# Half a sequence's six score units in one row, one pool of seven banks, and a shorter weight rounding, in a hash attention and SwiGLU kernel

## The chip, the cores and the metric

The kernel runs on one core of a Trainium2 chip. The metric is the device time of one execution in microseconds (us). The kernel before takes 1043.42 us, the median of three runs (1043.08 to 1043.81).

## What is computed

Attention over 4 batches, 8 heads, 768 positions and 64 dimensions, in which a query sees only the keys that fall into the same of 64 hash buckets (the signs of six projections). Its output, 3072 rows of 512, goes through a SwiGLU feed-forward block of 1536 hidden columns.

```python
q_bits = (np.einsum('bhsd,dk->bhsk', q, proj) > 0)
k_bits = (np.einsum('bhsd,dk->bhsk', k, proj) > 0)
mask = q_bucket[:, :, :, None] == k_bucket[:, :, None, :]   # bucket: the bits as a number
scores = np.where(mask, scale * np.matmul(q, k.transpose(0, 1, 3, 2)), -1e9)
attn = np.exp(scores - np.max(scores, axis=-1, keepdims=True))
attn = attn / (np.sum(attn, axis=-1, keepdims=True) + 1e-09)
x = np.matmul(attn, v)          # then (B, H, S, D) -> (B*S, H*D)
g = x @ w_gate
out = (g / (1 + np.exp(-g)) * (x @ w_val)) @ w_out
```

Inputs are fp32, but the three weight matrices come as 8-byte words (the double precision numbers as they are), and the kernel makes fp32 of them on the chip.

## The kernel before

**Attention.** The 32 (batch, head) pairs are taken two heads at a time: 16 *pairs*, four to a batch. A pair has two *halves* of 384 queries, and a half has six *units* of 128 keys (`units`, `NCH = 6`), so there are 192 units. For a unit `score(u)` issues four matmul groups: `kT` by `qT` in fp32 for each head (64 rows each, the two heads in two row tiles), and the hash bits `kb` by `qb` in bf16, which add a large negative number wherever the buckets differ. Two `exp` on ScalarE bring the two scores tiles into one of a ring of tiles `A`. `attend(u)` multiplies `v` by `A` (two heads in two 64-column tiles) and adds into one PSUM bank `av` over six units; after the sixth a copy on ScalarE (`avs`) frees it. `add(u)` adds the `A` tiles on VectorE into `acc`, five additions a half. `norm(u)` multiplies `acc` by ones (`sum`, which gives the sum over keys in every row), takes the reciprocal on VectorE, adds a small term `e` and writes the normalised `xT`.

**Front work of a pair.** `front(n)` yields eight steps: four transposes of `q` and `k` (TensorE, `tps`, then a copy on ScalarE) and four hash projections (`hps`, then a Sign on ScalarE and for `k` a scaling on VectorE). After the fourth pair VectorE transposes instead and one small set of matmuls makes all four projections.

**Weights.** `prepare()` is a generator of small VectorE steps that `prepare_on(count)` advances; every piece is 128 x 512 words, 36 pieces in all. `narrow(i)` turns a piece from doubles to fp32 in four VectorE steps: FLOOR (line 289), a shift (291), an integer addition (294) and the sign (297). With two of them it issues ScalarE steps for the next piece (`scalar_step`, lines 275 and 280), and with the last it asks GpSimd for the DMA of the words some pieces ahead (`load_words`). After every four pieces eight additions (line 325, `form`) make the sums that the fast multiplication needs.

**Feed-forward.** It uses Strassen's scheme (7 products instead of 8) on both multiplications. When the last pair of a batch is normalised, `push_ffn(b)` queues its *atoms*: sets of 14 `up` atoms (each one product for one of the gate and the value blocks of 256 hidden columns, added into one of the banks `a`, `b`, `c`), then chunks of seven `po` atoms for the second multiplication. Elementwise additions (`plus`) stand between them, and the first combinations of `xT` (`first`) are made on VectorE.

**Order.** The order is written out by hand: an engine does its instructions in the order in which the loops issue them. The first loop (units 0 to 47, the first four pairs, eight halves) goes by two units: score two, attend the two before, `norm` of a half that ended an iteration earlier, additions, two front steps, three preparation steps. There is no FFN work yet. The second loop (units 48 to 191, 24 halves) goes by half: score two, attend the four left over, four preparation steps, `norm` of the half before, score two, attend two, score two, and then 14 atoms of FFN work (or chunks of `po`) with additions, front steps and preparation steps between them. Weights are prepared until `MOVE` (unit 84).

**Banks and tiles.** PSUM has three pools: four banks for scores (`score_tile`; the `b` and `c` tiles of `up` and one `po` tile too), one for `av`, three for everything else (`bank`: transposes, hashes, sums, `up` and `po`). `A` is a ring of four tiles, six from unit 48 on.

Of the kernel before, what the change touches and what calls it, by code (L numbers as in the profile page):

```python
# [18 lines left out]
def kernel(  # L19
# [11 lines left out]
    nc = tc.nc  # L31
# [24 lines left out]

    FLOOR = 2.0**-15

    konst = ctx.enter_context(tc.tile_pool(name="konst", bufs=1))
# [6 lines left out]
    dram = ctx.enter_context(tc.tile_pool(name="dram", bufs=1, space=bass.MemoryType.DRAM))  # L66
    sc_ps = ctx.enter_context(tc.tile_pool(name="sc_ps", bufs=4, space=PSUM))
    av_ps = ctx.enter_context(tc.tile_pool(name="av_ps", bufs=1, space=PSUM))
    mm_ps = ctx.enter_context(tc.tile_pool(name="mm_ps", bufs=3, space=PSUM))

    ctx.enter_context(tc.manual_schedule())

    def bank(name):
        return mm_ps.tile([P, 512], FP32, tag="mm", name=name)

    def score_tile(name):
        return sc_ps.tile([P, 512], FP32, tag="sc", name=name)

# [80 lines left out]
    nc.vector.tensor_tensor(rules, rules, ident.unsqueeze(1).to_broadcast([P, 2, P]), op=ALU.mult)  # L159
    columns = konst.tile([P, 3], FP32, tag="columns", name="columns")  # L160
    nc.vector.tensor_reduce(out=columns[:, 0:2], in_=rules, axis=AX.X, op=ALU.add)
    nudge, times_k, two = (columns[:, x : x + 1] for x in range(3))
    nc.vector.memset(two, 2.0)

# [104 lines left out]

    def scalar_step(i, low):  # L270

        if i < len(pieces) and not low:
            nc.scalar.activation(pieces[i][0], words[i][:, :, 1].bitcast(FP32), AF.Abs)  # L275
        elif i < len(pieces):
            t = words[i]
            top = t.rearrange("p f w -> p (f w)").bitcast(U16)
            top = top.rearrange("p (f w) -> p f w", w=4)[:, :, 1]
            nc.scalar.activation(t[:, :, 0].bitcast(FP32), top, AF.Identity, bias=two,  # L280
                                 scale=2.0**-35 * (1 + 2.0**-17))

    def narrow(i):
        t, w = words[i], pieces[i][0]
        lo, hi = t[:, :, 0], t[:, :, 1]
        wi = w.bitcast(I32)


        nc.vector.tensor_single_scalar(w, w, FLOOR, op=ALU.max)
# [43 lines left out]
    def prepare():  # L333
        for n in range(2 * DF // PIECE):
            for j in range(NJ):
                if n + j == 0:
                    for low in (False, True):
                        scalar_step(0, low)
                yield from narrow(n * NJ + j)
            for pair in range(2):  # L340
                yield from form(n, pair)
        for f in range(NF):
            yield from narrow(2 * NJ * DF // PIECE + f)
        t2, t3, t4 = down_t
        for o, x, y, op in ((t3, b22, b12, ALU.subtract), (b12, b12, b11, ALU.subtract),
                            (t2, b22, b12, ALU.subtract), (t4, b21, t2, ALU.subtract)):
            while o is t4 and not progress["late"]:
                yield True
            for a in range(0, NFP, 2):
                nc.vector.tensor_tensor(o[:, a : a + 2], x[:, a : a + 2], y[:, a : a + 2], op=op)  # L350
                yield True
# [17 lines left out]

    def front_bank(name):  # L370

        return bank(name)

    def front(n):


        def transpose(name, half):
            if (name, n) not in T:
                T[name, n] = opnd.tile([P, S], FP32, tag=name + "T", name=name + "T")
            ps = front_bank("tps")  # L380
            for i in range(CH):
# [15 lines left out]
        def hash_bits(name, half):  # L397
            ps = front_bank("hps")
            nc.tensor.matmul(ps[:, 0:HQ], hash_w, T[name, n][:, half * HQ : (half + 1) * HQ],  # L399
# [5 lines left out]
        def hash_blocks():  # L405

            tile_ = front_bank("hps")
            for i, (name, half) in enumerate((name, half) for name in "kq" for half in range(2)):
# [39 lines left out]
    def weights(u):  # L448
        if u < LATE:
            return ring[u % RING]  # L450
        return ((early_ring if u < MOVE else late_ring) + ring)[(u - LATE) % (RING + 2)]

    def score(u):
        n, half, c = units[u]
        qs = slice(half * HQ, (half + 1) * HQ)
        ks = slice(c * P, (c + 1) * P)
        sc = [score_tile("sc")[:, 0:HQ] for _ in range(2)]
        for x, start in ((T, True), (bits, False)):
# [77 lines left out]
    def up_strassen(x, b, first):  # L536
# [14 lines left out]
        def both(i):  # L551
# [13 lines left out]
            def step(at):  # L565
                n, g = divmod(at, 2)
                my = now[g]
                if n == 0:
                    my["a"] = bank("up")[:, 0:HQ]
                    while first:  # L570
                        first.pop(0)()
                if at == 2:
                    for name in "cb":
                        for w in range(2):
                            now[w][name] = score_tile("up")[:, 0:HQ]
                block, to, xs = (
# [34 lines left out]
    def down_strassen(out_of):  # L611
# [22 lines left out]
        def chunk(i):  # L634
            now = {}

            def step(n):
                a11, a12, s3, a22 = parts(i, slice(None))
                if n == 0 and i == 0:
                    while next(preparing, None):  # L640
                        pass
                    for which in (1, 2, 3):
                        combine(0, which, 1)
                if n < 2:
                    now["ab"[n]] = bank("po")[:, 0:HD]
                elif n == 3:
                    now["c"] = score_tile("po")[:, 0:HD]
                if n == 0:
                    o = wraw.tile([P, PIECE, 2], I32, tag="words", name="o")
                    o = o.rearrange("p f w -> p (f w)").bitcast(FP32)  # L650
# [42 lines left out]


    steps = front(0)
    for _ in range(5):
        steps.pop(0)()
    N = len(units)
    per = 2 * NCH
    credit = ahead = 0.0  # L700
    left = []
    due = []
    for u in range(0, LATE, 2):
        n, at = divmod(u, per)
        if at == (4 if n == 0 else 0):
            steps.extend(front(n + 1))
        if at == per - 2:
            load(n + 2)
        score(u)
        score(u + 1)  # L710
        for x in left:
            attend(x)
        while due:
            norm(due.pop(0))
        for x in left:
            add(x)
            if units[x][2] == NCH - 1:
                due.append(x)
        left = [u, u + 1]
        for _ in range(2):  # L720
            if (u < 4 or u % per >= 2) and steps:
                steps.pop(0)()
        prepare_on(2 if u < 4 else 3)

    assert not steps
    for x in left:
        add(x)
    for u in range(LATE, N + NCH, NCH):  # L730
        if u < N:
            n, half, _ = units[u]
            if u == MOVE:
                progress["late"] = True
                for t in late_ring:
                    nc.gpsimd.memset(t[:, :, HQ:AW], 1.0)
            score(u)
            score(u + 1)
        for x in left:
            attend(x)  # L740
        prepare_on(4)
        ended = [x for x in due + left if units[x][2] == NCH - 1]
        due = []
        if u != LATE:
            for x in ended:
                norm(x)
        if u == N:
            break
        score(u + 2)
        score(u + 3)  # L750
        if u == LATE:
            for x in ended:
                norm(x)
        prepare_on(3)
        attend(u)
        attend(u + 1)
        score(u + 4)
        score(u + 5)
        prepare_on(4)
        add(u)  # L760
        add(u + 1)
        left = [u + c for c in range(2, NCH)]
        more = [lambda x=x: add(x) for x in left]
        if half == 0 and n + 1 < len(pairs):
            steps = front(n + 1)
            more[1:1] = [steps.pop(0)]
            more[3:3] = [steps.pop(0)]
        elif n + 1 < len(pairs):
            more[1:1] = [steps.pop(0)]
            if n + 2 < len(pairs):  # L770
                load(n + 2)
        chores = [lambda: first and first.pop(0)() and None for _ in first] + more

        credit += 14 if n < 2 * NP else 15.75
        end = True
        while atoms and (credit > 0 or not end):
            size, atom, end = atoms.pop(0)
            credit -= size
            atom()
            ahead += 0.85 * size  # L780
            prepare_on(int(ahead))
            ahead %= 1
            for _ in range(size):
                if chores:
                    chores.extend(chores.pop(0)() or [])
        while chores:
            chores.extend(chores.pop(0)() or [])
    for _, atom, _ in atoms:
# [33 lines left out]
```

## Time and profile before

| | |
|---|---|
| Median of three runs | 1043.42 us |
| The profiled execution | 1042.24 us |
| its span (first to last instruction) | 1040.5 us, so 1.74 us lie around it |
| TensorE clock granted | 0.998 of full speed |
| Reciprocal of the sum, VectorE | 32 x 2.56 us |
| Addition into `acc`, VectorE | 128 x 0.95 us |
| `exp` of one head's scores, ScalarE | 0.49 us each |

The page's second part divides the span into 40 slices of 26 us and gives each engine's busy share in tenths. Its fourth part follows the chain of work that ended last back from the end. Busy times are of one profiled execution. Matmuls overlap in their pipeline, so what a group of them costs is read best from one start to the next.

Five of the costliest groups, with busy time, mean duration in ns and, after the bar, the idle time before them:

```
L461 PE MATMUL sc<-qT,kT 64*128 64x384 f32 x768 | 168.0, 509 | 0.3
L464 ACT ACTIVATE A<-sc 128x384 f32<-128x384 f32 x288 | 120.8, 493 | 78.7 <-PE sc L461 62.6
L501 DVE RECIPROCAL r<-sum 128x384 f32<-128x384 f32 x32 | 81.8, 2556 | 103.9 <-PE sum L498 103.9
L488 DVE TENSOR_TENSOR acc<-acc,A 128x768 f32<-128x768 f32 x128 | 121.7, 951 | 6.4
L473 PE MATMUL av<-A,vraw 128*64 128x386 f32 x576 | 104.0, 496 | 0.0
```

### The profile page before, as it was taken

How to read it: one execution, taken by the hardware profiler on the slowest of the kernel's cores; microseconds unless marked ns; L12 is line 12 of the kernel's file. 1: busy time of each engine (PE TensorE's matmuls, PEld its weight loads, DVE VectorE, ACT ScalarE, POOL GpSimd, SP SyncE). 2: the span in 40 equal slices, each digit the busy share in tenths (PEclk: the TensorE clock that was granted, in tenths of full speed). 3: DMA queues.
4: the chain of work that ended last, by engine and by line, in shares of the span. 5: the costliest groups of instructions: out<-in, count | busy, mean ns of one | idle time of the engine just before them, and what ended most of it. 6: DMA issues, size and time to landing. Idle time of an engine off the chain costs nothing.

```text
span 1040.5 us, 12461 instructions
## 1 busy us (share of the span) xinstructions
PE 1029.3 (99%) x4597; PEld 604.8 (58%) x4597; DVE 628.9 (60%) x1044; ACT 424.2 (41%) x905; POOL 100.2 (10%) x192
## 2 busy tenths in 40 slices
PE   9999899999999999999999999999999999999998
PEld 4444345555456674555557666554545777555687
DVE  4899989989994435654566345455655442534521
ACT  7676637566542413534352422533535211222200
POOL 2122222221000000000000000000000000111000
PEclk9999999999999999999999999999999999999999
DMA  7565475865322122242411213241222000333101
GB/s 233 125 215 190 130 190 190 213 214 176 99 86 51 37 50 71 88 100 86 103 47 51 41 36 92 69 95 54 87 71 71 21 21 21 111 102 104 38 25 36
DMA packets 113885, 99.90 MB, mean 96 GB/s; under 512 B 86977, under 2 KB 97217, under 8 KB 113825
## 3 DMA queue, kind: packets, MB, share of 16 engines
q0 software_dynamic: 19104, 73.28, 22.0%
q1 hardware_dynamic: 93920, 25.64, 11.1%
q8 instruction: 36, 0.59, 0.2%
q10 hardware_dynamic: 800, 0.20, 0.1%
q14 instruction: 25, 0.20, 0.1%
HBM read 81.79 MB, written 17.30 MB: 95 GB/s over the span
## 4 chain that ended last, share of the span: by engine, by line
PE 90%; DVE 2%; DMA 0%; issue 0%; ACT 0%; ACTq 0%; DVEq 0%
PE up L530 42%; PE po L530 21%; PE sc L461 13%; PE av L473 11%; PE sum L498 2%; PE hps L409 1%; DVE r L501 1%; DMA words<-in_moe_w_val_dram 0%; DVE acc L488 0%; DVE room L325 0%; PE hps L399 0%; DVE acc L484 0%; PE tps L382 0%; DVE xT L504 0%; ACT A L464 0%
## 5 line engine op out<-in xcount | busy, mean ns | idle before, releaser
L530 PE MATMUL up<-xT,room 128*128 128x384 f32 x768 | 265.2, 492 | 4.2 <-ACT room L275 4.2
L530 PEld LDWEIGHTS up<-xT,room 128*128 128x128 f32 x768 | 144.5, 191 | 113.0 <-issue 7.9
L530 PE MATMUL up<-xc,room 128*128 128x384 f32 x576 | 197.5, 486 | 0.0
L461 PE MATMUL sc<-qT,kT 64*128 64x384 f32 x768 | 168.0, 509 | 0.3
L530 PEld LDWEIGHTS up<-xc,room 128*128 128x128 f32 x576 | 109.4, 190 | 76.3
L464 ACT ACTIVATE A<-sc 128x384 f32<-128x384 f32 x288 | 120.8, 493 | 78.7 <-PE sc L461 62.6
L501 DVE RECIPROCAL r<-sum 128x384 f32<-128x384 f32 x32 | 81.8, 2556 | 103.9 <-PE sum L498 103.9
L488 DVE TENSOR_TENSOR acc<-acc,A 128x768 f32<-128x768 f32 x128 | 121.7, 951 | 6.4
L534 DVE TENSOR_TENSOR c<-c,up 128x384 f32<-128x384 f32 x72 | 39.8, 553 | 138.3 <-PE up L530 138.0
L310 POOL DMA_DIRECT2D room<-ram x96 | 51.8, 540 | 689.6 <-PE up L530 678.2
L461 PEld LDWEIGHTS sc<-qT,kT 64*128 64x128 f32 x768 | 67.0, 186 | 72.6 <-issue 30.3
L473 PE MATMUL av<-A,vraw 128*64 128x386 f32 x576 | 104.0, 496 | 0.0
L662 ACT COPY o<-po 128x256 f32<-128x256 f32 x48 | 17.9, 372 | 191.9 <-PE po L530 191.9
L534 DVE TENSOR_TENSOR o<-o,po 128x256 f32<-128x256 f32 x36 | 15.2, 421 | 109.9 <-issue 51.5
L516 ACT ACTIVATE th<-c 128x384 f32<-128x384 f32 x72 | 37.6, 523 | 101.6 <-DVE c L534 101.4
L473 PEld LDWEIGHTS av<-A,vraw 128*64 128x64 f32 x576 | 37.1, 136 | 57.4 <-issue 56.0
L461 PE MATMUL sc<-qb,kb 64*128 64x384 bf16 x384 | 67.3, 323 | 0.2 <-DVE kb L394 0.2
L530 PE MATMUL po<-wo,hid 128*128 128x256 f32 x288 | 67.0, 382 | 0.0
L530 PE MATMUL po<-wo,room 128*128 128x256 f32 x288 | 66.3, 380 | 0.0
L530 PE MATMUL po<-room,hid 128*128 128x256 f32 x288 | 66.1, 379 | 0.0
L590 ACT COPY c<-up 128x384 f32<-128x384 f32 x72 | 34.4, 478 | 66.0 <-PE up L530 65.9
L530 PEld LDWEIGHTS po<-wo,hid 128*128 128x128 f32 x288 | 54.0, 190 | 11.6 <-DVE room L534 3.8
(112 smaller groups left out, 1033.3 us busy)
## 6 DMA issues: line engine op xcount, KB each, us to landing
room<-ram POOLq DMA_DIRECT2D x48, 512.0 KB, 4.6
room<-ram POOLq DMA_DIRECT2D x48, 384.0 KB, 4.0
vraw<-in_v_dram SPq DMA_DIRECT2D x16, 384.0 KB, 3.5
ram<-room POOLq DMA_DIRECT2D x12, 512.0 KB, 3.9
out_dram<-o SPq DMA_DIRECT2D x48, 128.0 KB, 1.7
qraw<-in_q_dram SPq DMA_DIRECT2D x48, 96.0 KB, 3.2
kraw<-in_k_dram SPq DMA_DIRECT2D x46, 96.0 KB, 3.3
words<-in_moe_w_out_dram POOLq DMA_DIRECT2D x8, 512.0 KB, 4.0
```

The source lines that it names most:

```text
L310: nc.gpsimd.dma_start(places[k % 2][:, PARTS[go], :], ram[k % NG][:, PARTS[go], :])
L461: nc.tensor.matmul(sc[h], x["k", n][rows, ks], x["q", n][rows, qs], start=start, stop=not start)
L464: nc.scalar.activation(weights(u)[:, h, 0:HQ], sc[h], AF.Exp, scale=SCALE)
L473: nc.tensor.matmul(ps[h * D : (h + 1) * D, 0:AW], raws["v", n][:, h, c, :], a[:, h, :], start=c == 0, stop=c == NCH - 1)
L488: nc.vector.tensor_tensor(acc[n, half], acc[n, half], a[:, :, 0:HQ], op=ALU.add)
L498: nc.tensor.matmul(ps[h * D : (h + 1) * D, 0:HQ], ones, t[:, h, :], start=True, stop=True)
L501: nc.vector.reciprocal(r, ps[:, 0:HQ])
L516: nc.scalar.activation(th, g, AF.Tanh, scale=0.5)
L530: nc.tensor.matmul(ps, a, x, start=start and i == 0, stop=i == len(pairs_) - 1, skip_group_check=True)
L534: nc.vector.tensor_tensor(o, a, b, op=op)
L590: nc.scalar.copy(tile_of(g, spot), c)
L662: nc.scalar.copy(o, c)
```

## The change

- **One loop for all units, by half.** A half's six `score` calls stand in a row with its additions between them, then its six `attend` calls, then preparation steps, then its own `norm`. In the first 48 units four front steps are spread before and after the `attend` calls and the preparation steps are eight (six in the very first half). From unit 48 on the atoms follow, with front steps and 0.7 preparation steps for each unit of atom size. No unit is scored ahead of the half before it any more, and none is attended in a later half.
- **Banks.** The pools of four and three banks become one pool of seven, from which every tile but `av` is taken. The six tiles of an `up` pair are all taken at its first atom, the three of a `po` chunk at its first.
- **Tiles `A`.** The ring has six tiles from the start, one for each unit of a half.
- **Weight rounding.** `narrow` has three VectorE steps (shift, sign, integer addition); FLOOR is gone. ScalarE has three steps instead of two for a piece: a scaled copy, an addition of 2^23 and a subtraction of it into an integer.
- **Loads.** `load(n + 2)` stands after the `attend` calls of a pair's second half.

The diff, cut:

```diff
-    sc_ps = ctx.enter_context(tc.tile_pool(name="sc_ps", bufs=4, space=PSUM))
     av_ps = ctx.enter_context(tc.tile_pool(name="av_ps", bufs=1, space=PSUM))
-    mm_ps = ctx.enter_context(tc.tile_pool(name="mm_ps", bufs=3, space=PSUM))
+    banks = ctx.enter_context(tc.tile_pool(name="ps", bufs=7, space=PSUM))
...
     def bank(name):
-        return mm_ps.tile([P, 512], FP32, tag="mm", name=name)
-
-    def score_tile(name):
-        return sc_ps.tile([P, 512], FP32, tag="sc", name=name)
+        return banks.tile([P, 512], FP32, tag="ps", name=name)
...
-    def scalar_step(i, low):
+    def scalar_step(i, k):
...
+        if k == 0:
+            nc.scalar.activation(w, t[:, :, 1].bitcast(FP32), AF.Copy, scale=2.0**-112)
+        elif k == 1:
+            nc.scalar.activation(lo.bitcast(FP32), top, AF.Identity, bias=whole,
+                                 scale=2.0**-13 * (1 + 2.0**-17))
+        else:
+            nc.scalar.activation(lo, lo.bitcast(FP32), AF.Identity, bias=unwhole)
...
-        nc.vector.tensor_single_scalar(w, w, FLOOR, op=ALU.max)
-        yield True
         nc.vector.tensor_single_scalar(wi, wi, 3, op=ALU.logical_shift_left)
-        scalar_step(i + 1, False)
-        yield True
-        nc.vector.tensor_tensor(wi, wi, lo, op=ALU.add)
-        scalar_step(i + 1, True)
+        scalar_step(i + 1, 0)
         yield True
         nc.vector.scalar_tensor_tensor(out=wi, in0=hi, scalar=-(1 << 31), in1=wi,
                                        op0=ALU.bitwise_and, op1=ALU.bitwise_or)
+        scalar_step(i + 1, 1)
+        yield True
+        nc.vector.tensor_tensor(wi, wi, lo, op=ALU.add)
+        scalar_step(i + 1, 2)
         load_words(i)
         yield True
...
     def weights(u):
-        if u < LATE:
-            return ring[u % RING]
-        return ((early_ring if u < MOVE else late_ring) + ring)[(u - LATE) % (RING + 2)]
+        return ((early_ring if u < MOVE else late_ring) + ring)[u % NCH]
...
-                if n == 0:
-                    my["a"] = bank("up")[:, 0:HQ]
+                if at == 0:
+                    for name in "cba":
+                        for w in range(2):
+                            now[w][name] = bank("up")[:, 0:HQ]
...
+    for u in range(0, N, NCH):
+        n, half, _ = units[u]
+        gating = u >= LATE
...
+        for c in range(NCH):
+            score(u + c)
+            if u == 0 and c in (1, 2, 4):
+                steps.pop(0)()
+            if c:
+                add(u + c)
+        if not gating:
+            if half == 0:
+                steps = front(n + 1)
+            for _ in range(2):
                 steps.pop(0)()
-        prepare_on(2 if u < 4 else 3)
...
+        for c in range(NCH):
+            attend(u + c)
+        if half == 1 and n + 2 < len(pairs):
+            load(n + 2)
+        if not gating:
+            for _ in range(2):
+                steps.pop(0)()
+        prepare_on(6 if u == 0 else 8)
+        norm(u + NCH - 1)
+        if not gating:
+            continue
+        chores = []
+        if n + 1 < len(pairs):
+            if half == 0:
+                steps = front(n + 1)
+                chores = [None, steps.pop(0), None, steps.pop(0)]
+            else:
+                chores = [None, steps.pop(0)]
...
-            ahead += 0.85 * size
+            ahead += 0.7 * size
             prepare_on(int(ahead))
```

More of the change, by code (lines that the diff above doesn't have):

```diff
@@ L55 @@
     EPS = 2.0**-100
-    FLOOR = 2.0**-15
     konst = ctx.enter_context(tc.tile_pool(name="konst", bufs=1))
@@ L159 @@
     nc.vector.tensor_tensor(rules, rules, ident.unsqueeze(1).to_broadcast([P, 2, P]), op=ALU.mult)
-    columns = konst.tile([P, 3], FP32, tag="columns", name="columns")
+    columns = konst.tile([P, 4], FP32, tag="columns", name="columns")
     nc.vector.tensor_reduce(out=columns[:, 0:2], in_=rules, axis=AX.X, op=ALU.add)
-    nudge, times_k, two = (columns[:, x : x + 1] for x in range(3))
-    nc.vector.memset(two, 2.0)
+    nudge, times_k, whole, unwhole = (columns[:, x : x + 1] for x in range(4))
+    nc.vector.memset(whole, 2.0**23)
+    nc.vector.memset(unwhole, -(2.0**23))
     hash_w = konst.tile([P, P], FP32, tag="hash", name="hash")
@@ L268, in load_words @@
             queue.dma_start(words[i].rearrange("p f w -> p (f w)"), pieces[i][1])
-    def scalar_step(i, low):
[L274 to L281, printed above, removed]
+    def scalar_step(i, k):
+        if i == len(pieces):
+            return
+        t, w = words[i], pieces[i][0]
+        lo = t[:, :, 0]
+        top = t.rearrange("p f w -> p (f w)").bitcast(U16).rearrange("p (f w) -> p f w", w=4)[:, :, 1]
+        if k == 0:
[5 more added lines that the diff above has]
+            nc.scalar.activation(lo, lo.bitcast(FP32), AF.Identity, bias=unwhole)
     def narrow(i):
@@ L336, in prepare @@
                 if n + j == 0:
-                    for low in (False, True):
-                        scalar_step(0, low)
+                    for k in range(3):
+                        scalar_step(0, k)
                 yield from narrow(n * NJ + j)
@@ L368 @@
     first = []
-    def front_bank(name):
-        return bank(name)
     def front(n):
@@ L379, in transpose @@
                 T[name, n] = opnd.tile([P, S], FP32, tag=name + "T", name=name + "T")
-            ps = front_bank("tps")
+            ps = bank("tps")
             for i in range(CH):
@@ L397, in hash_bits @@
         def hash_bits(name, half):
-            ps = front_bank("hps")
+            ps = bank("hps")
             nc.tensor.matmul(ps[:, 0:HQ], hash_w, T[name, n][:, half * HQ : (half + 1) * HQ],
@@ L405, in hash_blocks @@
         def hash_blocks():
-            tile_ = front_bank("hps")
+            tile_ = bank("hps")
             for i, (name, half) in enumerate((name, half) for name in "kq" for half in range(2)):
@@ L456, in score @@
         ks = slice(c * P, (c + 1) * P)
-        sc = [score_tile("sc")[:, 0:HQ] for _ in range(2)]
+        sc = [bank("sc")[:, 0:HQ] for _ in range(2)]
         for x, start in ((T, True), (bits, False)):
@@ L567, in step @@
                 my = now[g]
-                if n == 0:
-                    my["a"] = bank("up")[:, 0:HQ]
+                if at == 0:
+                    for name in "cba":
+                        for w in range(2):
+                            now[w][name] = bank("up")[:, 0:HQ]
                     while first:
                         first.pop(0)()
[L572 to L575, printed above, removed]
                 block, to, xs = (
@@ L643, in step @@
                         combine(0, which, 1)
[L644 to L647, printed above, removed]
                 if n == 0:
+                    for name in "cba":
+                        now[name] = bank("po")[:, 0:HD]
                     o = wraw.tile([P, PIECE, 2], I32, tag="words", name="o")
@@ L698 @@
     N = len(units)
-    per = 2 * NCH
     credit = ahead = 0.0
[L701 to L707, printed above, removed]
-            load(n + 2)
[L709 to L721, printed above, removed]
-                steps.pop(0)()
-        prepare_on(2 if u < 4 else 3)
@@ L727 @@
[L727 to L772, printed above, removed]
@@ new lines @@
+    for u in range(0, N, NCH):
+        n, half, _ = units[u]
+        gating = u >= LATE
+        if u == MOVE:
+            progress["late"] = True
+            for t in late_ring:
+                nc.gpsimd.memset(t[:, :, HQ:AW], 1.0)
+        for c in range(NCH):
[12 more added lines that the diff above has]
+        if half == 1 and n + 2 < len(pairs):
+            load(n + 2)
+        if not gating:
+            for _ in range(2):
+                steps.pop(0)()
+        prepare_on(6 if u == 0 else 8)
[9 more added lines that the diff above has]
+                chores = [None, steps.pop(0)]
@@ L784 @@
                 if chores:
-                    chores.extend(chores.pop(0)() or [])
+                    step = chores.pop(0)
+                    chores.extend(step and step() or [])
         while chores:
-            chores.extend(chores.pop(0)() or [])
+            step = chores.pop(0)
+            chores.extend(step and step() or [])
     for _, atom, _ in atoms:
```

## The prediction

> **What bounds the kernel now.** I read the page first (shares and slices), then the waits of TensorE in two windows, then the chain of waits and the timelines around one late and one early stretch. From the page:
>
> ```profile
> PE 1029.3 (99%) x4597; PEld 604.8 (58%) x4597; DVE 628.9 (60%) x1044; ACT 424.2 (41%) x905; POOL 100.2 (10%) x192
> PE   9999899999999999999999999999999999999998
> DVE  4899989989994435654566345455655442534521
> ACT  7676637566542413534352422533535211222200
> PE 90%; DVE 2%; DMA 0%; issue 0%; ACT 0%; ACTq 0%; DVEq 0%
> ```
>
> TensorE is the bound, but VectorE stands at 80 to 90% from the second slice to the twelfth (26 us each, so to 312 us), while weights are prepared; after that only TensorE is full. The list of waits says how long TensorE stood: nothing from 160 us to the end, and in 0 to 160 us only this:
>
> ```profile
> PE up L530 <- ACT room L275: 4.2, 1, 4.2
> PE sum L498 <- DVE acc L488: 1.9, 2, 1.6
> ```
>
> So after 160 us a microsecond less of TensorE's own work is a microsecond less of time. What a half costs TensorE is in the chain of waits at 186 to 222 us:
>
> ```profile
> 207.12 1.82 PE sc L461 x12
> 208.93 2.74 PE av L473 x16
> 211.68 0.65 PE sum L498 x4
> 212.32 1.82 PE sc L461 x12
> 214.14 1.45 PE av L473 x8
> 215.58 1.82 PE sc L461 x12
> ```
>
> Scores (sc, two 64-row tiles) and value products (av, two 64-column tiles) alternate: 10.30 us a half in six blocks. The timeline of TensorE shows the price of a change between them:
>
> ```profile
> 207.04 0.92 PE L461 MATMUL sc<-qT,kT 64*128 64x384 f32 x4
> 207.79 0.33 PE L461 MATMUL sc<-qb,kb 64*128 64x384 bf16 x2
> 207.96 0.81 PE L461 MATMUL sc<-qT,kT 64*128 64x384 f32 x4
> ```
>
> By starts, the first unit's four fp32 matmuls take 0.75 (207.04 to 207.79), the second's 0.64 (207.96 to 208.60): about 0.10 on entering a mode, and as much on leaving (the last bf16 pair takes 0.26 instead of 0.17). A unit inside a row costs 0.81; four av units took 2.64, two 1.44.
>
> **What the Trainium skill says.** "TensorEngine Tiling (Array Packing)", Tiling Modes, Key Properties: changing the tiling mode drains TensorE. The trace agrees, at 0.10 us a boundary. "TensorE: Matmul & The Clock Gate", Part 1, What's actually happening: after an idle window of about 3.4 us the clock falls to half and needs work to come back. The trace agrees: after 4.23 us idle at 125 us eight `up` matmuls took 4.27 instead of 2.74 (about 1.5 lost). "ScalarE: Activation LUTs", What ACT_TABLE_LOAD costs: an activation is 186 ns + 0.833 per element of a row, about 93 ns more for each pointer operand, and back to back they overlap by 93 ns. For 512 columns that gives estimates of 0.61 and 0.71; the trace has 0.68 and 0.777 (started 0.57 and 0.66 apart). "Perfetto Trace Analysis", Tensor Engine Instruction, has ScalarE and VectorE as strict first-in first-out; no out-of-order start shows here.
>
> **The change part by part.**
>
> *Rows of six, second stage.* Six scores in a row are 6 × 0.81 + 0.20 = 5.06 instead of 3 × 1.82 = 5.46; six av are 6 × 0.65 + 0.04 = 3.94 instead of 2.64 + 1.45 = 4.09 (the sum uses the av mode). Together 0.55 a half. Would a new wait eat it? Seven banks hold three units; the fourth needs the first unit's exps. ScalarE's exp repeats every 0.405, twice a unit: 0.81, just TensorE's pace. Scores end at T+5.1, exps at about T+6.1, the five adds (0.935 each) at T+7.6, while the sum comes at T+9.1: covered by 1.5 us. The sum's bank goes next to a c tile of `up` at atom 6 or 7, 8 us later (atoms are 1.29): its reciprocal is covered. Without that cover each half would pay the difference. The same atoms and chunks follow each half, so the end is the same. 23 halves after the first of this stage: 23 × 0.55 = **-12.65**.
>
> *Weight rounding.* 36 pieces lose the FLOOR step (0.42): -15.1 us of VectorE, 8 of it or so before 160 us. They gain a third ScalarE step, 128x512 in fp32 with one pointer operand. The nearest rows give 0.57 to 0.68; I take 0.62: +22 us of ScalarE. After 312 us neither runs; between 160 and 312 ScalarE is at 30 to 70%, and TensorE did not wait there. In the first stage the steps sit in a different place, next.
>
> *First stage (eight halves, no FFN work).* Before, a pair costs TensorE 26.3 us (sums at 40.48, 66.81, 93.34), scores run two units ahead of the value products, and three preparation steps follow every two units. After, a half is: six scores with adds, two front steps, six value products, two front steps, eight preparation steps, sum. TensorE's own work falls to 11.7 (transposes, 4 × 0.42) and 13.1 (hashes, 4 × 0.75) a half, 24.8 a pair. VectorE's per pair: ten adds 9.35, two reciprocals 4.94, xT and e 1.3, kb 0.5, sixteen steps averaging 0.53 (a cycle of twelve narrowing steps at 0.62 and eight forming steps at 0.40) 8.5: 24.6. Two engines equally full, now with work in lumps. Two couplings follow, which the profile of before shows in a mild form:
>
> ```profile
> 67.54 0.42 DVE L289 TENSOR_SCALAR room<-room 128x512 f32<-128x512 f32 x1
> 67.88 2.55 DVE L501 RECIPROCAL r<-sum 128x384 f32<-128x384 f32 x1
> 70.34 0.10 DVE L503 TENSOR_SCALAR e<-avs 128x1 f32<-128x1 f32 x1
> 70.49 0.62 DVE L504 SCALAR_TENSOR_TENSOR xT<-avs,e,r 128x384 f32<-128x384 f32 x1
> ```
>
> The reader sees that the reciprocal waits its turn (its sum was issued at 66.81) and holds the sum's bank until 70.4. First, in the changed program that bank is the one which the fifth score unit of the next half, or a transpose, waits for, and the reciprocal is behind five adds and eight steps: T+7.6, +5.0, +2.5 = T+15.1, against a need at T+11.7+3.3 = T+15.0. Even when nothing else is late it is only just in time. Second, ScalarE is in order: behind the last front copies (PE reaches them at T+10.5) stand up to nine scalar steps of 0.6, until about T+16, then the next half's exps, wanted at T+12.8. The fourth score unit, which needs the first unit's banks, is about 2.6 late in halves of narrowing steps, and not late in halves of forming steps: over the cycle (12 of 20 steps) about 1.6 a half. Carrying both through the eight halves by hand, I get sums at 26.3, 43.0, 56.5, 70.6, 85.4, 98.7, 112.1, 127.7: 14.5 a half, against 13.3 before. Moved to the same point of work (before has four more units scored and two attended ahead, 5.1 us), before's are 22.0 to 115.3. So +4.3 at the first sum (the transposes of pair 1 now stand before the first value products and wait for q of pair 1, a DMA issued after 12 us that lands near 19; load(n+2), later now, has a whole half of slack) and +8.1 over the next seven halves: +12.4.
>
> *Passage to the FFN.* Before, the first FFN stalls on weight words and an add:
>
> ```profile
> 129.69 4.27 PE L530 MATMUL up<-xT,room 128*128 128x384 f32 x8 [4.23 <-ACT room L275]
> 153.39 0.87 PE L498 MATMUL sum<-acc,ones 128*64 128x384 f32 x4 [1.60 <-DVE acc L488]
> ```
>
> After, the last sum's reciprocal is behind eight steps and followed by the combinations that the second product needs: about 6.4 idle and 1.5 of slow clock, against 4.23 + 1.5 + 1.60. From 127.7: 11.7 to the next half's sum (9.75 of work, 2 for late exps), 0.75 for it, 18.06 for the 14 products, 7.9 for the stall, 0.5 for words not yet there: 166.6, where before's equivalent is 152.3 (154.19 less the two units scored and attended ahead). The 12.4 is in this: **+14.3** (8 if ScalarE's order costs half of what I assume, 20 if words arrive 2 to 5 us late).
>
> *Rest of the preparation, five halves.* Eight steps before the norm, then 0.7 an atom, ScalarE some 10% fuller with the third step, and atom copies in the same line as steps that wait for words; 0 to 5, I take **+2.5**. *Pool, ring of six A tiles, load moved, two more columns*: nothing beyond this, hidden under TensorE; for queueing on SP and POOL I add 0.5 (0 to 1).
>
> Sum: 14.3 - 12.65 + 2.5 + 0.5 = +4.65 on the profiled 1042.24 (span 1040.5 and 1.74 around it): 1046.9. The median of the runs is 1.18 above the profiled execution: **1048**.
>
> **Rivals.**
> A, faster: early halves keep the old 13.3 (VectorE sheds 8 us there, and TensorE has less to do), so the loss is 4.3 and about 2 at the passage, and the later preparation costs nothing: +6.3 - 12.65 + 0.5 = -5.9, about 1037.5. For it: both engines' sums per pair fall below 26.3. Against it: lumps, and one order on ScalarE. It decides from where the stall per half is below the 1.5 that TensorE saved per pair.
> B, no change: half of coupling two, so +8 early, +2 at the passage, +2.5 and 0.5 later: about 1043.8.
> C, much slower: the five preparation halves also stall 2.5 each, as ScalarE's line holds atom copies behind steps waiting for words (such a wait is in before, 2.98 us at 128.95), with clock loss: +10, about 1058.
> D: the exps do not keep TensorE's pace in rows of six (0.81 to 0.81): 0.3 a half over 24, +7, about 1055. Against it: before's exps had 62.6 us of waiting for scores.
>
> **How the numbers follow.** Forecast 0.46 (its own range 1045.6 to 1052), A 0.17, B 0.16, C 0.16, D 0.05. About 0.2%, 2.1 us, is what can be told from no change. A is faster, B within it, the others slower: 0.17, 0.16, 0.67. The range 1039 to 1057 leaves out the lower part of A and the upper part of C.
>
> **What would show it.** Right: rows of sc near 5.06 and av near 3.94 after 250 us, no TensorE wait there; before 140 us waits of sc for exps (A) and for the reciprocal, 1 to 3 us each; sums 14 to 15 apart; a stall of 5 to 8 at the first `up` atoms. Wrong: sums 13 apart (A), stalls at atoms between 170 and 240 us (C), rows of sc over 5.3 (D).

## The result: 1053.77 us, about 10 us slower

The changed kernel takes 1053.77 us (median of four runs, 1053.15 to 1054.13), the kernel before 1043.62 in the same comparison. The ratio is 1.0092, with a 95% interval of 1.0074 to 1.0109. The direction was as forecast, the size was not: 4.6 us were expected, 10.2 came. 1053.77 still lies in the wide range of the prediction (1039 to 1057), but above the forecast's own (1045.6 to 1052).

The page of the changed kernel's profiled execution (1054.13 us, span 1052.3) gives these lines, in tenths for 40 slices of 26 us and, last, the shares of the chain that ended last:

```profile
PE 1021.5 (97%) x4597; PEld 615.2 (58%) x4597; DVE 623.6 (59%) x1009; ACT 446.6 (42%) x941; POOL 99.1 (9%) x192
PE   8898869999999999999999999999999999999998
PEclk8999989999999999999999999999999999999999
PE 89%; ACT 4%; DVE 4%; DMA 1%; issue 1%; SPq 0%; DVEq 0%; ACTq 0%; POOLq 0%
```

TensorE was busy 7.8 us less than before (1029.3), although the clock was slow for part of that time: it has less to do, as intended. The loss is in the first six slices, where it is idle and where the clock shows two eights. From the seventh slice on the page looks as before. The list of TensorE's waits in the first 160 us has these three largest holes (total, times, longest):

```profile
PE sc L452 <- ACT room L455: 11.5, 5, 3.6
PE up L521 <- DVE xT L525: 7.1, 1, 7.1
PE tps L375 <- DMA qraw<-in_q_dram: 3.4, 1, 3.4
```

The kernel before had 6.1 us of such waits there, 1.9 for additions and 4.2 for a rounding step. (A wait of 1.3 us at the very start, which the prediction's list left out, stands in both kernels.) Now 11.5 us are waits of scores for `exp`.

**Where the time went, stretch by stretch.** The FFN atoms come in the same order in both kernels, so the times of their groups' ends can be set side by side. The first 14 atoms end at 172.56, against 152.3 for the same work before (154.19, where its half has its sum, less 1.9 for two units that it has scored ahead; the prediction's "and attended" is a slip): +20.3, good to about 0.3. At the end of the sixth half with atoms (319.88 against 294.70, less the 3.4 us of value products and sum that the kernel before still owes there) the difference is 21.8. At the end it is 11.8, so the last 18 halves gave 10.0 back, 0.56 each. A steady half on TensorE's timeline:

```profile
172.49 0.92 PE L452 MATMUL sc<-qT,kT 64*128 64x384 f32 x4
177.54 1.52 PE L464 MATMUL av<-room,vraw 128*64 128x386 f32 x8
181.48 0.81 PE L489 MATMUL sum<-acc,ones 128*64 128x384 f32 x4
182.22 2.85 PE L521 MATMUL up<-xT,room 128*128 128x384 f32 x8
```

By the starts, six scores take 5.05, six value products 3.94 and the sum 0.74, as worked out.

**What the waits are.** ScalarE's timeline ahead of the second half's exps (seven more rounding steps, of the same three kinds, stand between the second and the third line):

```profile
28.01 0.48 ACT L378 COPY qT<-tps 128x384 f32<-128x384 f32 x1
28.38 0.68 ACT L275 ACTIVATE room<-hid 128x512 f32<-128x512 f32 x1
...
33.74 0.75 ACT L280 ACTIVATE hid<-hid,columns 128x512 int32<-128x512 f32 x1
34.39 1.61 ACT L455 ACTIVATE room<-sc 128x384 f32<-128x384 f32 x4
```

Nine rounding steps run from 28.38 to 34.4, and the half's first `exp` only then, although TensorE began its scores at 28.65. With three units scored, in six of the seven banks, TensorE stood 3.57 us until the first unit's exps had freed theirs:

```profile
31.01 0.33 PE L452 MATMUL sc<-qb,kb 64*128 64x384 bf16 x2
34.91 1.16 PE L452 MATMUL sc<-qT,kT 64*128 64x384 f32 x3 [3.57 <-ACT room L455]
```

**And what came after the waits.** Windows of four microseconds, with the span and busy time of TensorE first, then the other engines, and the granted clock third from the right:

```profile
20.00:24.00 4.00, 4.00 (x14) 1.68 (x15) 0.00 (x0) 0.96 (x2) 0.00 (x0) 0.50 0.02 4
36.00:40.00 4.00, 4.00 (x17) 2.75 (x15) 3.69 (x5) 2.95 (x8) 0.00 (x0) 0.63 0.25 98
52.00:56.00 4.00, 4.00 (x17) 3.01 (x17) 3.46 (x4) 3.27 (x9) 0.47 (x1) 0.58 0.43 154
156.00:160.00 4.00, 4.00 (x10) 2.29 (x9) 4.00 (x8) 1.46 (x3) 0.10 (x1) 0.70 0.00 0
```

TensorE is fully "busy" there, at 50 to 70% of its clock. A busy digit does not show this; the clock does. Four microseconds at 0.50 lose 2.0 of full-speed work. With the neighbouring windows, the waits at 19.3, 34.9 and 51.8 us cost 2.6, 1.7 and 1.7 more than themselves: 6.0 us together. Set against the same matmuls at full clock later in the run it is 2.9, 1.7 and 1.7.

### The profile page after: what moved, and what is told of

It is laid out like the page before. It is cut to its first block, busy times and chain, and to the rows that moved or that the text cites. A ratio compares the mean times of both kernels' runs of the same rounds, so it can differ in the third digit from the quotient of the medians.

```text
span 1052.3 us, 12423 instructions
## 1 busy us (share of the span) xinstructions
PE 1021.5 (97%) x4597; PEld 615.2 (58%) x4597; DVE 623.6 (59%) x1009; ACT 446.6 (42%) x941; POOL 99.1 (9%) x192
## 4 chain that ended last, share of the span: by engine, by line
PE 89%; ACT 4%; DVE 4%; DMA 1%; issue 1%; SPq 0%; DVEq 0%; ACTq 0%; POOLq 0%
PE up L521 39%; PE po L521 21%; PE sc L452 13%; PE av L464 12%; PE sum L489 1%; PE hps L392 1%; DVE r L492 1%; PE hps L402 1%; ACT room L275 1%; DMA qraw<-in_q_dram 1%; PE tps L375 1%; DVE room L322 1%; ACT hid L277 1%; DVE acc L479 0%; ACT qb L385 0%
## 5 line engine op out<-in xcount | busy, mean ns | idle before, releaser
L452 PE MATMUL sc<-qT,kT 64*128 64x384 f32 x768 | 166.6, 502 | 12.6 <-ACT room L455 11.5
L452 PEld LDWEIGHTS sc<-qT,kT 64*128 64x128 f32 x768 | 74.5, 189 | 67.8 <-issue 46.0
L455 ACT ACTIVATE A<-sc 128x384 f32<-128x384 f32 x256 | 105.6, 496 | 5.1 <-PE sc L452 5.0
L464 PE MATMUL av<-A,vraw 128*64 128x386 f32 x512 | 89.4, 491 | 0.0
L452 PE MATMUL sc<-qb,kb 64*128 64x384 bf16 x384 | 71.0, 327 | 0.2 <-DVE kb L387 0.2
L455 ACT ACTIVATE room<-sc 128x384 f32<-128x384 f32 x128 | 53.7, 488 | 33.5 <-PE sc L452 33.5
```

Source lines behind the costliest of these rows:

```text
L452: nc.tensor.matmul(sc[h], x["k", n][rows, ks], x["q", n][rows, qs], start=start, stop=not start)
L455: nc.scalar.activation(weights(u)[:, h, 0:HQ], sc[h], AF.Exp, scale=SCALE)
L464: nc.tensor.matmul(ps[h * D : (h + 1) * D, 0:AW], raws["v", n][:, h, c, :], a[:, h, :], start=c == 0, stop=c == NCH - 1)
```

## Experiments

Theory S says: the lump of ScalarE rounding steps (up to nine in a row) stands, in ScalarE's order, ahead of the next half's exps, TensorE runs out of banks, and the slow clock adds to it. Rival R: the sum's bank, which waits for a reciprocal behind eight preparation steps on VectorE. Rival L: rows of six without a unit scored ahead stall TensorE whatever else is done.

| Run | median us | ratio to before (95%) |
|---|---|---|
| the change | 1053.77 | 1.0092 (1.0074 to 1.0109) |
| e1 preparation right after the scores | 1036.42 | 0.9935 (0.9918 to 0.9951) |
| e2 norm ahead of the preparation | 1055.10 | 1.0120 (1.0105 to 1.0135) |
| e3 old first loop, new second loop | 1039.10 | 0.9965 (0.9953 to 0.9976) |
| e4 the change with the old rounding | 1057.05 | 1.0140 (1.0119 to 1.0162) |
| e5 e1, combinations early | 1035.57 | 0.9920 (0.9891 to 0.9948) |
| e6 e5, first half's front steps later | 1032.39 | 0.9889 (0.9874 to 0.9904) |
| e7 before with the new rounding alone | 1040.61 | 0.9971 (0.9959 to 0.9983) |
| e8 e6 with the two old pools | 1062.42 | 1.0167 (1.0144 to 1.0189) |
| e9 e6, preparation after unit 48's atoms | 1026.54 | 0.9840 (0.9825 to 0.9854) |
| e10 e9 with the old rounding | 1033.66 | 0.9909 (0.9893 to 0.9926) |
| e11 e9 with the row broken once | 1035.26 | 0.9923 (0.9908 to 0.9938) |
| e12 the change, first half's front steps later | 1049.32 | 1.0070 (1.0052 to 1.0088) |

The runs come from several comparisons, whose medians for the kernel before lie between 1042.80 and 1043.62 us. Differences below between runs of different comparisons are therefore good to about 0.8 us.

**e1, the lump moved.** Nothing else changes:

```diff
         if not gating:
+            prepare_on(6 if u == 0 else 8)
             if half == 0:
                 steps = front(n + 1)
...
-        prepare_on(6 if u == 0 else 8)
+        if gating:
+            prepare_on(8)
         norm(u + NCH - 1)
```

> In the first eight halves the preparation steps stand right after the six scores, ahead of the front steps and value products, so that their ScalarE steps run beside the value products. Theory S (ScalarE's order: the lump of scalar steps stands ahead of the next half's exps, TensorE waits for banks, and the clock falls after the longest of these waits): the waits of sc for exps in 28 to 125 us (11.5 us in all) fall below 3, the slow clock at 36 and 53 us goes, and the time falls by 8 to 12, to 1042 to 1046. Rival R (the sum's bank, held until the reciprocal, which stands behind the preparation on VectorE): its place there is the same, so within 2 of 1053.8. Rival L (rows of six with nothing scored ahead stall TensorE in any order of the rest): a fall of less than 3, with the waits merely renamed.

It took 17.4 us off, more than S had put. 1.5 of it is there at the first sum already. From the first sum to the eighth it is 14.0 us faster (90.6 for 104.6): 8.9 less of waits (2.9 for 11.8 between 28 and 125 us) and the 3.4 of slow clock behind two of them; the other 1.7 was not traced. The next half, of unit 48, takes 9.8 for 12.0. S had reckoned with the waits and the clock alone. L falls, and so does R as the cause of the loss. VectorE's part of the preparation moved along with ScalarE's here; e2 and e4 look at VectorE by itself. TensorE's waits between 28 and 125 us are now only these:

```profile
PE sc L452 <- DVE e L494: 1.7, 3, 1.0
PE sc L452 <- ACT avs L468: 1.2, 1, 1.2
```

The reciprocal is still in its old place (the first line is its wait: `e` comes right behind it), and costs 1.7 in all. The rounding steps now run while TensorE multiplies values, where it needs little of ScalarE.

**e2, the reciprocal moved.**

```diff
-        prepare_on(6 if u == 0 else 8)
+        if gating:
+            prepare_on(8)
         norm(u + NCH - 1)
+        if not gating:
+            prepare_on(6 if u == 0 else 8)
```

> In the first eight halves the norm, with its reciprocal, is issued ahead of the preparation steps; the order on ScalarE is the same. Theory S: the waits for exps stay, the time falls by 0 to 3. Rival R: the reciprocal is 5 us earlier in each half, the waits go, and the time falls by 7 or more, below 1047. Rival L: as S.

The time did not fall (1055.10; its interval overlaps the changed kernel's). The waits for exps stay in part (7.6 in the same window), and in the first 175 us 3.9 of waits for additions have taken the place of the rest. The reciprocal's place is not what binds here.

**e3, the old first loop in front of the new second one.** Its body, left out here, is that of the kernel before.

```diff
+    for u in range(0, LATE, 2):
...
+        prepare_on((u // 2 + 1) * 8 // 3 - u // 2 * 8 // 3)
...
+    for x in left:
+        attend(x)
+        add(x)
+    norm(LATE - 1)
-    for u in range(0, N, NCH):
+    for u in range(LATE, N, NCH):
```

> The first 48 units run by the old loop (two units ahead, 8/3 preparation steps every two units), with the new rounding, the one pool and six A tiles; from unit 48 the new loop. S and L: no lumps and two units ahead, so TensorE does not wait before 115 us and sums stand about 13.3 apart; with the 0.55 a half kept in the second stage the time is 1030 to 1036. If the new rounding or the one pool is what costs in the first stage, it stays above 1043.

The first stage is as expected: sums at 27.11, 40.52, 54.05, 66.77, and 1.4 us of waits between 2 and 117 us. The one pool, the six tiles and the new rounding are in this run too, so what costs in the first stage is the order. But the time is 1039.10, above the 1030 to 1036 expected, because the seam between the two loops was left out of account. Emptying the look-ahead at unit 48 makes the last sum wait 4.84 us for additions, with 1.7 of slow clock behind it, and then comes the wait for the combinations of `xT` that the changed kernel has too:

```profile
118.01 1.08 PE L489 MATMUL sum<-acc,ones 128*64 128x384 f32 x4 [4.84 <-DVE acc L479]
138.97 4.54 PE L521 MATMUL up<-xT,room 128*128 128x384 f32 x8 [5.94 <-DVE xT L525]
```

**e4, the old rounding in the changed order.** `narrow` and `scalar_step` are those of the kernel before, and the steps a half are 10 or 11.

> The changed kernel with the old rounding (four VectorE steps, two ScalarE steps a piece) and 10 to 11 preparation steps a half for 8. S: the lump on ScalarE shrinks from 9 steps (5.5 us) to some 5 (3.1 us), the wait at 34.9 us from 3.57 to about 1.5 and the clock no longer falls there, VectorE's queue ahead of the reciprocal grows by 0.9: the time falls by 3 to 8. If the third ScalarE step costs nothing, the time is the same or up to 5 longer (longer VectorE queue, rival R).

Here S's number was wrong: 1057.05, 3.3 above the changed kernel, which is what the other alternative had put. The list of waits (first 175 us) says why:

```profile
PE sc L453 <- DVE e L495: 7.0, 3, 2.5
PE sum L490 <- DVE acc L480: 6.4, 4, 3.3
PE sc L453 <- ACT room L456: 3.3, 3, 1.3
```

The waits for exps fell from 11.5 to 3.3 as S has it, but VectorE, with ten steps in place of eight, took their place at the reciprocal and the additions. So rival R's wait exists, behind the other: with the third ScalarE step the lump is on ScalarE, without it on VectorE, where it costs more.

**e5 and e6, the holes at 140 and 19 us.** e5 adds to e1 that at unit 48 the first combinations are issued right after the scores. e6 adds that in the first half the four front steps of pair 1 stand after the value products, so that these do not wait for `q` of pair 1.

```diff
+        if u == LATE:
+            while first:
+                first.pop(0)()
...
-            for _ in range(2):
+            for _ in range(2 if u else 0):
                 steps.pop(0)()
...
-            for _ in range(2):
+            for _ in range(2 if u else 4):
                 steps.pop(0)()
```

> As e1_prep_first, and at unit 48 the combinations of batch 0's xT are issued right after the six scores, ahead of the preparation steps and the half's own reciprocal. Theory S: the wait of up for xT (6.6 us in e1) goes, and with it the slow clock behind it (0.89 and 0.94 in 120 to 160 us, some 2 us): 7 to 9 below e1, 1027 to 1030. Rival (weight words or the blocks' DMA are late there as well, as in the kernel before): a wait for ACT or a DMA of 3 to 6 us takes its place and the fall is under 4.

> As e5_combine_early, and in the very first half the four front steps of pair 1 stand after the six value products, so that these run while q of pair 1 is on its way. Theory S with the clock: the wait of 2.9 at 19 us goes and the slow clock of 20 to 27 us (2 to 2.5 lost) with it: 3 to 5 below e5. If the clock costs nothing by itself: 2 to 3. If the next half is late anyway (front copies and scalar steps then stand ahead of its exps): under 1.

e5's rival was right: the wait for `xT` went, and one of 5.5 us for a copy on ScalarE came in its place. The median says little here, since e5's four executions lie in two pairs: 1032.94 and 1033.13 at a mean granted clock of 0.997, 1038.01 and 1038.14 at 0.993. The profiled one is of the first pair; in it the wait at 19 us, 2.95 long, left the clock at 1.00. In e6 that wait is gone, and its four lie between 1031.86 and 1032.73: 0.6 below the first pair and 5.7 below the second. A clock that falls behind this wait in one execution and not in another would explain a part (e1's profile shows 1.7 us lost there), but not the 5.0 us between the pairs; the second pair has no profile, and where it lost stays open. The copy's wait is still there in e6, and ScalarE's timeline shows it standing behind rounding steps that wait for weight words:

```profile
125.45 0.78 ACT L280 ACTIVATE room<-room,columns 128x512 int32<-128x512 f32 x1
131.03 0.66 ACT L275 ACTIVATE room<-words 128x512 f32<-128x512 f32 x1 [4.80 <-DMA words<-in_moe_w_val_dram]
...
134.47 0.47 ACT L579 COPY c<-up 128x384 f32<-128x384 f32 x1
```

**e9, those steps moved past the atoms.**

```diff
-        if gating:
+        if gating and u != LATE:
             prepare_on(8)
         norm(u + NCH - 1)
...
+        if u == LATE:
+            prepare_on(8)
         while chores:
```

> As e6_first_half, and at unit 48 the eight preparation steps stand after the 14 atoms, so that no ScalarE step that waits for weight words stands ahead of the atoms' first copies. Theory S: the wait of up for the copy c (6.0 us) falls below 1.5 and the slow clock behind it goes: 6 to 9 below e6, 1023 to 1026. Rival (words are late in any order, the wait moves to a later half of the preparation): less than 3 below e6, with new waits of up between 150 and 300 us.

The 6.0 us wait is gone, the clock stays at 1.00 in every 20 us window to 180 us, and the time is 1026.54: 5.9 below e6, a little less than expected, 27.2 below the changed kernel. It beats the kernel before by 1.6% (ratio 0.9840, 0.9825 to 0.9854). The three largest of TensorE's waits that are left in the whole span:

```profile
PE up L521 <- ACT c L579: 2.2, 3, 1.1
PE sc L452 <- DVE e L494: 1.7, 3, 1.0
PE idle L134 <- DVE kb L131: 1.3, 1, 1.3
```

**e7 and e10, the rounding by itself.** e7 is the kernel before with the new rounding and three quarters of the preparation steps; e10 is e9 with the old rounding and four thirds of them.

> The kernel before with the new rounding alone, its preparation steps scaled by three quarters. TensorE waited only 6 us there for anything but its own work, so the rounding alone should move the time by -2 to +3; S: 1041 to 1046. If the shorter VectorE work were what the change lives on, it would fall by more than 3; if the third ScalarE step were what it loses by, it would rise by more than 5.

> As e9_passage, with the old rounding (four VectorE and two ScalarE steps a piece) and the preparation steps scaled by four thirds. With the lumps out of the way, S gives the rounding -1 to +5 (VectorE's longer queue ahead of the reciprocal in the first eight halves). If the shorter rounding were worth its 15 us of VectorE on the path: 8 or more above e9.

The new rounding is a gain in both orders: 3.0 us in the old one, more than the -2 to +3 that was expected and just short of the bound for "what the change lives on", and 7.1 in e9's, between the two expectations. e10 waits for the reciprocal and the scaled hash bits, both on VectorE (4.0 and 4.7 us), so in a first stage whose lumps are out of the way VectorE's work is on the path in part.

**e8, the two old pools.** e6 with four banks for scores and three for the rest.

```diff
-        sc = [bank("sc")[:, 0:HQ] for _ in range(2)]
+        sc = [score_tile("sc")[:, 0:HQ] for _ in range(2)]
```

> As e6_first_half, with the old pools of four and three banks and the old places where the up and po tiles are taken. Two units fit in the scores' banks where three did: if the row needs the third, TensorE waits 0.3 to 0.5 for an exp in each row and the time is 5 to 12 above e6; if not, the same within 2.

It is 30.0 above e6, far more than expected. In the chain of waits (start, duration, what) a row now takes 5.83, where it took 5.05:

```profile
627.10 5.83 PE sc L456 x30
632.93 4.04 PE av L468 x24
636.98 0.65 PE sum L493 x4
```

Other rows in this trace take 5.72 to 5.83, so it is 0.7 to 0.8 a half, 16 to 19 for 24. The list of waits has none of it after 340 us: it shows in the starts. The rest is in the first 340 us, with waits of hashes for the reciprocal's bank (`hps` for `e`, 7.4 us in three) and a clock of 0.83 to 0.91 in three windows; its parts were not separated. A row of six needs the third unit's banks.

**e11, the row broken once.**

```diff
             if c:
                 add(u + c)
+            if gating and c == 3:
+                attend(u)
+                attend(u + 1)
...
-        for c in range(NCH):
+        for c in range(2 if gating else 0, NCH):
             attend(u + c)
```

> As e9_passage, and in the 24 halves with FFN work the row is broken once: four scores, two value products, two scores, four value products. If the gain of the second stage is the number of changes between the score and value modes, one more block of each costs 0.20 + 0.15 = 0.35 a half, in all 8.4 (7 to 10). If the gain came from elsewhere (one pool, adds, the order of chores), it costs under 2.

8.72 us more, or 0.36 a half where 0.35 was expected. In the chain of waits a half at 601 us takes 3.43 and 1.82 for its scores and 1.45 and 2.74 for its value products, 9.44, where e9's order gives 5.05 and 4.04, and TensorE waits 1.5 us in all after 250 us. So the gain of the second stage is the number of changes between the modes of scores and of value products.

**e12, the first hole alone.** The changed kernel with e6's edit to the first half.

> The changed kernel with one edit: in the very first half the four front steps stand after the six value products. The wait of 3.41 us at 19.3 us goes. If the slow clock behind a wait is a term of its own (2.6 us lost between 19 and 28 us by the granted clock), the first sum comes 5 to 6 us earlier (27.85 to about 22) and the time falls by 4 to 6, to 1048 to 1050, the second half's wait for exps and its slow clock staying. If the clock costs nothing beside the wait: the first sum about 24.4, a fall of 2 to 3.5. If the next half is the bound in any case: a fall under 1.5.

4.45 us less in the median; the four executions scatter from 1047.52 to 1052.02, all below the changed kernel's lowest, and why they scatter is not shown. In the profiled one, the fastest, the first sum comes 6.5 us earlier (changed kernel first):

```profile
27.85 0.87 PE L489 MATMUL sum<-acc,ones 128*64 128x384 f32 x4
```

```profile
21.33 0.87 PE L489 MATMUL sum<-acc,ones 128*64 128x384 f32 x4
```

The work ahead of it is the same, and the wait that went was 3.41 us long, so the slow clock behind it is a term of its own, of some 3 us. The seventh half's sum is still 6.5 earlier (110.76 for 117.28): neither was hidden.

## Why the prediction was wrong in size

- **Rows of six, -12.65: right.** 0.55 a half was predicted, 0.56 measured over the last 18 halves, and e11 shows the cause.
- **Coupling two, ScalarE's order: right.** "About 2.6 late in halves of narrowing steps" met waits of 3.57, 1.68, 2.89, 1.71 and 1.63. From the first sum to the eighth the prediction had 101.4, the profile has 104.6.
- **The step that failed: the first-stage sums, 26.3 to 127.7, were carried through at full clock.** The prediction quoted the slow clock behind 4.23 us of idle time and charged 1.5 for it once, at the passage. It charged nothing for the waits of the first halves, although it had them itself: +4.3 at the first sum, 2.6 in a half of narrowing steps. The windows show 6.0 there, 3.4 of it between the first and the eighth sum: the difference between 104.6 and 101.4 to within 0.2. So this stretch, with what follows up to the 14th atom, came to +20.3 for +14.3. That this excess is 6.0 too is in part chance: 1.5 of it is at the first sum, where 2.6 of clock was lost, 3.2 between the first and the eighth, and 1.2 in the passage, whose clock was charged. e12 shows one such place by itself.
- **Coupling one, the reciprocal: exists, costs little.** The prediction had it just in time and 0.3 us is its wait between 28 and 125 us. e2 moved it and gained nothing; e4 shows it when ScalarE is not in front of it.
- **Passage: right in kind.** Predicted 6.4 idle, 0.5 for words and 1.5 of clock; measured 7.1 idle and 1.6 of clock, and the scores and the sum ahead of it were 0.4 slower than reckoned. Its cause was named rightly too: e5 took the wait for `xT` away. What was late next, atom copies behind steps that wait for words, had been put down to the later halves.
- **Rest of the preparation, +2.5: too small.** From the first 14 atoms to the sixth half with atoms the difference grew by 1.5 while the rows gave back 2.8: 4.3 lost. TensorE's waits explain 2.3 of it (most for the copies `c` and `hid`, 0.5 to 0.9 each); the other 2 were not tracked down. The 0.5 for queueing was not seen.
- **Rounding: costed at nothing beyond ScalarE's lump, but a gain.** e7, e4 and e10 give 3.0, 3.3 and 7.1 us for it in three orders.
- **Rivals.** D's 1055 and C's 1058 stand as near to the result as the forecast or nearer, but not for their reasons: rows at 5.05, where D needs over 5.3, and 2.3 us of waits in the five preparation halves, where C has 2.5 in each. A and B expected a smaller loss in the first stage.

In sum: +20.3, +4.3 and 23 times -0.56 make 11.7, against 11.8 in the spans and +4.65 predicted.

## What to carry to other kernels

Where an engine works in order, ask what stands ahead of the next stage's first instruction on every engine that feeds the bound one: here the same preparation steps cost 17 us less beside the value products than ahead of the exps. When a prediction puts a wait of three microseconds or more on TensorE, add the slow clock behind it (here 1.5 to 3 us each), and read the clock by short windows, since busy time hides it. A batch that saves changes of mode needs enough banks to run ahead of its evictions. And a first stage can lose more than a second one gains: here 24.6 us, with the rest of the preparation, against 12.9.

## What was not expected of the hardware

The length of a wait does not by itself decide on the clock. In the changed kernel a wait of 1.68 us at 51.8 was followed by a clock of 0.58, and behind one of 2.89 us at 81.4 the clock stayed full. In e12 a wait of 1.66 us in the same place of the program left the clock at 1.00, as these two windows show (changed kernel first):

```profile
80.00:84.00 4.00, 2.63 (x17) 2.07 (x18) 3.95 (x5) 4.00 (x11) 0.53 (x1) 1.00 0.74 244
```

```profile
45.00:49.00 4.00, 3.63 (x24) 2.70 (x24) 3.95 (x5) 4.00 (x12) 1.07 (x2) 1.00 0.56 202
```

The Trainium skill ("TensorE: Matmul & The Clock Gate", Part 1, What's actually happening) speaks of an idle window of about 3.4 us. The drops behind 3.41, 3.57 and 7.1 us agree; the one behind 1.68 does not. Over the fourteen profiles of this case all 17 waits of TensorE of 3.28 us and more were followed by slow clock, so were six of ten between 2.63 and 2.95 us (one of 2.88 in e1, not one of 2.95 in e5), and of 16 between 1.50 and 2.46 us only that one of 1.68. What decides below 3 us was not settled here.
